# Attention steps taken by twos: which half of the TensorE array scores and value products use, and how often they trade

## The chip, the core and the metric

The kernel runs on one core of a Trainium2 chip. The metric is device time in microseconds (us) of one execution of the whole program. The time of the kernel before is the median of three runs, 1683.56 us (1682.72 to 1688.05).

## What is computed

One transformer block over 2048 tokens of width 512: a layer norm modulated by a condition vector, attention with 32 query heads of 16 dimensions that share a single key head and a single value head, a residual, a second modulated layer norm, a gated feed-forward layer of width 1792, and a second residual. The part that the change touches is the attention:

```python
q = (x @ wq).reshape(B, S, H, Dh).transpose(0, 2, 1, 3)
k = x @ wk
v = x @ wv
scores = jnp.einsum("bhqd,bkd->bhqk", q, k) * (Dh ** -0.5)
p = _softmax(scores, axis=-1)
o = jnp.einsum("bhqk,bkd->bhqd", p, v)
```

## The kernel before

**Stages.** A prologue (a plan of tokens, `PLAN`) makes the modulation vectors, the first layer norm, keys, values and the first queries. Then comes the main loop. Then a tail does what is left of the feed-forward layer on the whole array.

**The main loop** (lines 1106 to 1155) runs over 32 units, each a block of 256 queries by one group of 8 heads, and inside a unit over 16 steps `kb`, one for each tile of 128 keys. There are 512 steps, and each step has two halves, `n` = 0 and 1: 1024 half-steps. A half-step issues, in the order `ORDER` (line 57) and then a piece:

- `a0`, `a1`: two score tiles (PSUM tile `sa`, line 584) with queries along partitions, for a later unit. VectorE takes the row maximum of each into `mx` (line 599). The maxima later go into the query tile as an extra row, so that the exponentials can't overflow.
- `s0`, `s1`: two score tiles (PSUM tile `st`, line 634) with keys along partitions. ScalarE takes the exponential of each into `P` (line 642).
- `c`: the products of `P` with `V` (line 647), of a key tile two steps back (`vq`, `LAG` = 2). They gather over all 16 key tiles of a unit in one PSUM bank, `craw`.
- `piece` (line 1095): a few products of the rest of the block (queries `pq`, output projection `po`, gate and up `pgu`, down `pd`), handed out by `plan` and `places`.

**The array's two row sets.** Nearly all matmuls of the main loop use the TensorE array in 8 parts: 2 row sets (partitions 0 to 63 and 64 to 127) by 4 sets of 32 columns. The function `columns` (line 145) issues four matmuls, one for each set of columns. The row set comes from where the operands lie: `kp[64 * j:64 * j + 64]` in `a_product` (line 590) and `st_tile` (line 640), and `V[rs, t, :]` with `rs = slice(64 * j, 64 * j + 64)` in `pv` (lines 650 and 655). For a score tile `j` says which four of the eight heads it is. For a product with `V`, `j` says which 64 of the tile's 128 keys it adds up, so a product needs the score tiles of both `j`. A piece (`Couple.part`) uses both row sets, first the one that `pv` did not use last.

In the loop, `h` is taken from `sides(kb)`: the scores of a half-step use row set `1 - h`, and `pv` uses `sides(t)[second]` with its own, older key tile `t`.

**The exchange.** The matmuls that gather in `craw` come from both row sets, and one row set may only add to the bank when the other has finished. So after the products of one row set `hand_over` (line 159) issues a matmul of one column of zeros (`nought`) which raises the semaphore `turn`, and before the products of the other row set `take_over` (line 169) waits for it. Before the change this is done inside every step, between its two halves, and in the middle of every piece group.

Of the kernel before, what the change touches and what calls it, by code (L numbers as in the profile page):

```python
# [9 lines left out]
F32 = mybir.dt.float32  # L10
# [6 lines left out]
P = 128  # L17
# [38 lines left out]
A0 = 84  # L56
ORDER = "a0", "s0", "c", "a1", "s1"
LAG = 2
# [24 lines left out]
PBUFS = 4  # L83
# [6 lines left out]
def adaln_mqa_glu_kernel(  # L90
# [36 lines left out]
    def sbank(name):  # L127
        return psum["s"].tile([P, 512], F32, tag=name, name=name, bufs=psum["banks"][name])
# [16 lines left out]
    def columns(dst, l_, r_, start, stop):  # L145
        for c_ in range(0, P, 32):
            pe.matmul(dst[c_:c_ + 32], l_[:, c_:c_ + 32], r_, start=start, stop=stop)

    turn, done, side, open_ = nc.alloc_semaphore("turn"), [0], [0], [False]
# [4 lines left out]
    def behind(later, earlier):  # L154
        tc.add_manual_dep(later.ins, earlier.ins.name,
                          mybir.DependencyInfo(mybir.DependencyClass.Sync, mybir.DependencyReason.DATA),
                          reason="a bank that Tile doesn't follow")

    def hand_over():
        g, rs = 32 * (done[0] // 2 % 4), slice(64 * side[0], 64 * side[0] + 64)  # L160
        z = pe.matmul(raw_c["c"][g:g + 32, 0:1], nought[rs], nought[rs, 0:1], start=False, stop=False)
        if not done[0]:
            behind(z, nought_set)
        done[0] += 1
        z.then_inc(turn, 1)
        tc.add_to_no_dep_group("turn", z.ins)
        tc.no_tile_sem_insts.add(z.ins.name)

    def take_over(since=None):
        pe.wait_ge(turn, done[0] if since is None else since)  # L170
# [20 lines left out]
    class Couple:  # L191
# [3 lines left out]
        def part(self, n0, n1):  # L195
            if n0 == 0:
                for g in self.gs:
                    g.open()
            m = self.gs[0].n
            for n in range(n0, n1):  # L200
                if n == m:
                    take_over(self.since)
                for j in (1 - side[0], side[0]):
                    g = self.gs[j ^ (n >= m)]
                    l_, r_, *cut = g.term(n % m, slice(64 * j, 64 * j + 64))
                    columns(cut[0](g.bank) if cut else g.bank, l_, r_, n == 0, n == 2 * m - 1)
                if n == m - 1:
                    self.since = None
                    if open_[0]:
                        hand_over()  # L210
                        self.since = done[0]
            if n1 == self.n:
                for k, g in enumerate(self.gs):
                    g.end(g.bank, k == 1)
# [335 lines left out]
    P_ = {}  # L550
# [19 lines left out]
    def get_q(i):  # L570
        if i not in qps:
            b, o = units[i]
            assert (b * QU // QB, o) in qdone
            load_q(i)
        return qps[i]


    def sides(t):
        return (0, 1) if t % 2 == 0 else (1, 0)

    def spot(n):
        return n // 16, n // 8 % 2, n % 2, n // 2 % 4

    def a_product(i, n):
        qp = get_q(i)
        if i not in mxs:
            mxs[i] = wp.tile([P, 8, 2, 4], F32, tag="mx", name="mx", bufs=2)
        kc, qt, j, r = spot(n)
        sa = sbank("sa")
        l_, r_ = qp[64 * j:64 * j + 64, r, qt * P:(qt + 1) * P], kp[64 * j:64 * j + 64, kc * 512:(kc + 1) * 512]  # L590
        if first:
            pe.matmul(sa, l_, r_, start=True, stop=True)
        else:
            columns(sa, l_, r_, True, True)
        return i, n, sa

    def a_max(i, n, sa):
        kc, qt, j, r = spot(n)
        dve.tensor_reduce(mxs[i][:, 4 * j + r, qt, kc:kc + 1], sa, axis=AX.X, op=ALU.max)
        if i > 0 and n == 62:  # L600
            pend.append((i,))

    def a_tile(i, n):
        a_max(*a_product(i, n))

    pend = []

    def max_end(i):
        m16 = wp.tile([64, 32], F32, tag="m16", name="m16", bufs=4)
# [24 lines left out]
    def st_tile(i, t, pr, j, second):  # L634
        qp = get_q(i)
        if not second:
            P_[pr] = P2.tile([P, 2, 512], F32, tag=f"P{pr}", name=f"P{pr}", bufs=PBUFS)
        p_ = P_[pr]
        s_ = sbank("st")
        columns(s_, kp[64 * j:64 * j + 64, t * P:(t + 1) * P], qp[64 * j:64 * j + 64, 2 * pr:2 * pr + 2].rearrange("p r q -> p (r q)"),  # L640
                True, True)
        act.activation(p_[:, j], s_, AF.Exp, scale=0.25)
        Ps[i, t, 2 * j + pr] = p_[:, j]
# [3 lines left out]
    def pv(i, t, second):  # L647
        c_ = raw_c["c"]
        side[0] = j = sides(t)[second]
        rs = slice(64 * j, 64 * j + 64)  # L650
        start, stop = t == 0 and not second, t == NKB - 1 and second
        if second:
            take_over()
        for hh in range(4):
            z = pe.matmul(c_[32 * hh:32 * hh + 32, :], V[rs, t, :], Ps[i, t, hh][rs, :], start=start, stop=stop)
            if start and hh == 0 and i > 0:
                behind(z, raw_c["out"])
        open_[0] = not stop
        if not second:
            hand_over()  # L660
        raw_c["last"] = z
        if second:
            for hh in range(4):
                del Ps[i, t, hh]
            if stop:
                unit_end(i)
# [51 lines left out]
    for g in range(8):  # L718
        p_, r_, j = g // 4, g // 2 % 2, g % 2
# [65 lines left out]
    class Transposes:  # L785
        stage, n = "tr", 4

        def __init__(self, part, u):
            self.part, self.u = part, u
# [171 lines left out]
    alist = [(i, n) for i in range(len(units)) for n in range(64)]  # L961
# [32 lines left out]
    for tok in PLAN.split():  # L994
        name = tok.rstrip("0123456789")
# [8 lines left out]
    P2 = ctx.enter_context(tc.tile_pool(name="w2", bufs=1, reuse_waits="tile"))  # L1004
# [40 lines left out]
    def ready(pair, gs, i):  # L1045
        for g in gs:
            g.ready = i * NKB
        return [(pair, g) for g in gs]
# [54 lines left out]
    vq = []  # L1103
    lows = []

    for i, (b, o) in enumerate(units):
        if o == 0 and b == NQ - 1:
            ends = ffn_groups(NB - 1)
            first_rows.append(Couple(*ends[0][:2]))
        if o == 0 and b % 2 == 1 and b < NQ - 1:  # L1110
            blocks[b // 2] = ffn_groups(b // 2)
            wos, trs, _, es = blocks[b // 2]
            main.extend([*ready(b // 2, [Couple(*wos[:2]), trs[0], trs[2]], i), (None, len(es)), *ready(b // 2, es, i)])
        if o == 0 and b % 2 == 0 and b > 0:
            wos, trs, gs, _ = blocks.pop(b // 2 - 1)
            gs = [Couple(*wos[2:]), trs[1], trs[3], *gs]
            main.extend([*ready(b // 2 - 1, gs[:-KEPT], i), (None, KEPT), *ready(b // 2 - 1, gs[-KEPT:], i)])
        for kb in range(NKB):
            s = i * NKB + kb
            now[0] = s  # L1120
            if kb == NKB - QLEAD - 5 and i + 2 < len(units):
                get_q(i + 2)
            late, pend[:] = pend[:], []
            for z in [z for z in waits if z[0] <= s]:
                waits.remove(z)
                z[1]()
            rows = [max_end(*z) for z in late]
            an = A0 + 4 * s

            old, lows[:] = lows[:], []  # L1130
            for n, h in enumerate(sides(kb)):
                for z in ORDER:
                    k = int(z[1:] or 0)
                    if z[0] == "a" and an + 2 * k + 1 - h < len(alist):
                        a_tile(*alist[an + 2 * k + 1 - h])
                    if z == "c" and len(vq) >= LAG:
                        pv(*vq[0], n == 1)
                    if z[0] == "s":
                        st_tile(i, kb, k, 1 - h, n == 1)
                if n == 1:  # L1140
                    lows.extend(z() for z in rows)
                piece(s, n)
                if n == 0:
                    for z in old:
                        z()
            if len(vq) >= LAG:
                vq.pop(0)
            vq.append((i, kb))
            while wdone < nw:
                if wdone < nw - 4 and (wdone + 0.5) * WSTEPS > (s + 1) * (nw - 4):  # L1150
                    break
                if wdone >= nw - 4 and s < WLAST + 3 * (wdone - nw + 4):
                    break
                wjobs[wdone]()
                wdone += 1
    assert wdone == nw and len(qdone) == 4 * NB
    while run:
        piece(s, 1)
    while vq:
        for n in range(2):  # L1160
            pv(*vq[0], n == 1)
        vq.pop(0)
    while waits:
        now[0] += 1
        for z in [z for z in waits if z[0] <= now[0]]:
# [54 lines left out]
```

## Time and profile before

| | |
|---|---|
| median of the runs, us | 1683.56 |
| the profiled execution: its own time, us | 1685.55 |
| the profiled execution: span from first to last instruction, us | 1683.7 |
| mean granted TensorE clock | 0.99 |
| share of the span busy: PE, DVE, ACT, POOL | 98%, 85%, 77%, 36% |

PE is TensorE, DVE VectorE, ACT ScalarE, POOL GpSimd; PEld is the loading of weights into the array. A row of the timeline gives the start, the length until the last of its instructions ended, the engine, the line, the operation, the tiles written and read, the shape and how many instructions follow each other. A shape like `64*32` ahead of the operand is the part of the array that a matmul uses. A matmul's length has its way through the array in it, so how long a row set is taken is read from the distance of starts, not from the lengths. All matmuls of the helper stand under line 136.

### The profile page before, as it was taken

To read this page: it belongs to the slowest core of one execution; us is meant where nothing else is said; L and a number is where in the kernel's file an instruction comes from. 1 tells how busy PE (TensorE), PEld (TensorE's weight loads), DVE (VectorE), ACT (ScalarE), POOL (GpSimd) and SP (SyncE) were. 2 spreads that over 40 slices of the span, in tenths; PEclk is the share of its full clock that TensorE was granted. 3 is DMA by queue.
4 is the path that set the end of the run, shared out by engine and by line. 5 is a ranking of instruction groups with operands and counts; after the bars stand their busy time and mean duration, and the time that the engine had idled before them with its cause. 6 is when DMAs were issued, how large, how long until landed. Compare 5 with 4: busy or idle time off the path is not lost.

```text
span 1683.7 us, 87854 instructions
## 1 busy us (share of the span) xinstructions
PE 1644.5 (98%) x39747; PEld 974.6 (58%) x39747; DVE 1430.9 (85%) x2428; ACT 1295.4 (77%) x2335; POOL 610.5 (36%) x784
## 2 busy tenths in 40 slices
PE   6999999999999999999999999999999999999998
PEld 3335445454456666666656666666666666654443
DVE  7789999999999999999999999999999999912311
ACT  5548889888888888888888888888888888884100
POOL 4432445475033442222543232223543333132423
PEclk9989999999999999999999999999999999999999
DMA  7111333331011120101021110100121110011211
GB/s 242 57 62 28 103 114 96 98 96 40 21 61 41 57 70 15 41 28 28 28 77 53 47 45 15 41 24 27 38 78 49 45 53 16 24 47 52 88 51 38
DMA packets 86722, 94.05 MB, mean 56 GB/s; under 512 B 24916, under 2 KB 65868, under 8 KB 86348
## 3 DMA queue, kind: packets, MB, share of 16 engines
q1 hardware_dynamic: 86348, 88.44, 17.0%
q8 instruction: 311, 5.10, 1.2%
q14 instruction: 63, 0.52, 0.1%
HBM read 67.82 MB, written 16.24 MB: 50 GB/s over the span
## 4 chain that ended last, share of the span: by engine, by line
PE 83%; DVE 11%; ACT 2%; issue 1%; DMA 1%; POOL 0%; SPq 0%; POOLq 0%; ACTq 0%; DVEq 0%
PE craw L136 23%; PE sa L136 16%; PE pgu L136 14%; PE st L136 10%; DVE mx L136 9%; PE pd L136 6%; PE pgu L187 5%; PE pd L187 3%; PE po L136 2%; PE pq L136 2%; ACT P L136 1%; DMA xall<-in_A_x_dram 1%; ACT th L136 1%; DVE h2h L136 1%; DVE st L136 1%
## 5 line engine op out<-in xcount | busy, mean ns | idle before, releaser
L136 DVE TENSOR_REDUCE mx<-sa 128x1 f32<-128x512 f32 x2048 | 1291.5, 682 | 64.0 <-PE sa L136 29.1
L136 ACT ACTIVATE P<-st 128x512 f32<-128x512 f32 x2048 | 1175.2, 598 | 197.2 <-PE st L136 133.6
L136 PE MATMUL craw<-P,V 64*32 64x512 f32 x8192 | 1088.0, 598 | 0.2
L136 PE MATMUL sa<-kp,qp 64*32 64x512 f16 (+1 forms) x7940 | 826.6, 378 | 10.5 <-DVE mx L136 9.8
L136 PE MATMUL st<-qp,kp 64*32 64x512 f16 x8192 | 831.8, 379 | 4.8 <-ACT P L136 4.5
L136 PEld LDWEIGHTS <-kp 64*32 64x32 f16 x8192 | 323.9, 91 | 254.5 <-issue 102.2
L136 PEld LDWEIGHTS <-qp 64*32 64x32 f16 (+1 forms) x7940 | 284.4, 92 | 166.5 <-issue 82.4
L136 PE MATMUL pgu<-h2h,gw 64*32 64x512 f16 x5248 | 273.8, 376 | 1.0
L136 PEld LDWEIGHTS <-gw 64*32 64x32 f16 x7872 | 175.0, 92 | 59.4 <-issue 16.2
L136 PEld LDWEIGHTS craw<-P,V 64*32 64x32 f32 x8192 | 184.5, 105 | 15.0 <-issue 2.0
L136 PE MATMUL pgu<-h2l,gw 64*32 64x512 f16 x2624 | 165.3, 376 | 0.3 <-POOL h2l L357 0.3
L901 POOL TENSOR_SCALAR th<-th 128x512 f32<-128x512 f32 x41 | 25.4, 620 | 356.0 <-ACT th L136 300.2
L136 PE MATMUL craw<-nought 64*32 64x1 f16 x571 | 93.1, 163 | 0.0
L557 POOL MEMSET qp<- 32x1024 f16 x60 | 56.7, 945 | 83.3 <-PE st L136 80.8
L321 POOL TENSOR_SCALAR wst<-wst 128x512 f32<-128x512 f32 x46 | 28.5, 621 | 144.7 <-DMA wst<-in_B_w_up_dram 89.4
L187 PE MATMUL pgu<-h2h,gw 128*128 128x512 f16 x240 | 71.9, 379 | 1.5 <-DVE h2h L356 1.5
L136 PEld LDWEIGHTS <-nought 64*32 64x32 f16 x571 | 53.1, 93 | 34.2 <-issue 28.8
L895 ACT ACTIVATE th<-pgu 128x512 f32<-128x512 f32 x15 | 9.0, 597 | 82.1 <-PE pgu L187 82.1
L136 PE MATMUL pd<-wdh,gh 64*32 64x512 f16 x1152 | 70.4, 376 | 0.6 <-DVE t L136 0.2
L136 PE MATMUL pd<-wdl,gh 64*32 64x512 f16 x1152 | 70.3, 376 | 0.0
L136 PE MATMUL pd<-wdh,gl 64*32 64x512 f16 x1152 | 69.7, 376 | 0.0
L136 DVE COPY u<-pgu 128x512 f32<-128x512 f32 x41 | 28.0, 682 | 48.6 <-PE pgu L136 48.4
(160 smaller groups left out, 1426.8 us busy)
## 6 DMA issues: line engine op xcount, KB each, us to landing
gw<-wD SPq DMA_DIRECT2D x56, 512.0 KB
wD<-gw SPq DMA_DIRECT2D x14, 512.0 KB
wm<-in_w_mod_dram SPq DMA_DIRECT2D x6, 1024.0 KB
qp<-qD SPq DMA_DIRECT2D x192, 32.0 KB
qD<-q SPq DMA_DIRECT2D x16, 256.0 KB
xr<-in_A_x_dram SPq DMA_DIRECT2D x16, 256.0 KB
out_dram<-ot SPq DMA_DIRECT2D x16, 256.0 KB
raw<-cs SPq DMA_DIRECT2D x248, 16.0 KB
```

Source lines behind the costliest of these rows:

```text
L136: return (lambda *a, **k: keep(f_(*a, **k))) if pinned else f_
L187: pe.matmul(cut[0](self.bank) if cut else self.bank, l_, r_, start=(n == 0), stop=(n == self.n - 1))
L321: pool.tensor_scalar(w_, w_, SW, 0.0, op0=ALU.mult, op1=ALU.add)
L557: eng.memset(qp[j:j + 32], 0.0)
L895: act.activation(th, p_, AF.Tanh, scale=0.5 / (SH * SW))
L901: pool.tensor_scalar(th, th, 1.0, 1.0, op0=ALU.add, op1=ALU.mult)
```

## The change

Steps go by pairs. A step now issues one row set's scores for both key tiles of its pair (one tile in each half-step), and the next step the other row set's. The products with `V` do the same with the two key tiles of the pair before. The function `sides` turns over with each pair of steps where it turned over with each step. There is one exchange for each pair of steps, and one more at each unit's first product. The number of score tiles, exponentials, maxima, products and pieces is as before.

```diff
                 if n == m:
+                    assert self.since is not None or done[0] > self.marks
                     take_over(self.since)
...
                 if n == m - 1:
-                    self.since = None
+                    self.since, self.marks = None, done[0]
...
     def sides(t):
-        return (0, 1) if t % 2 == 0 else (1, 0)
+        return (0, 1) if t // 2 % 2 == 0 else (1, 0)
...
-        if i > 0 and n == 62:
+        seen[i] = seen.get(i, 0) + 1
+        if i > 0 and seen[i] == 64:
             pend.append((i,))
...
-            P_[pr] = P2.tile([P, 2, 512], F32, tag=f"P{pr}", name=f"P{pr}", bufs=PBUFS)
-        p_ = P_[pr]
+            P_[t % 2, pr] = P2.tile([P, 2, 512], F32, tag=f"P{pr}", name=f"P{pr}", bufs=PBUFS)
+        p_ = P_[t % 2, pr]
...
         side[0] = j = sides(t)[second]
         rs = slice(64 * j, 64 * j + 64)
         start, stop = t == 0 and not second, t == NKB - 1 and second
-        if second:
+        if second and t % 2 == 0:
             take_over()
...
         open_[0] = not stop
-        if not second:
+        if start or not second and t % 2 == 1:
             hand_over()
...
-            an = A0 + 4 * s
+            an = A0 + 4 * (s - kb % 2)
+            second = kb % 2 == 1
+            h = sides(kb)[second]
 
             old, lows[:] = lows[:], []
-            for n, h in enumerate(sides(kb)):
+            for n in range(2):
+                t = kb - kb % 2 + n
                 for z in ORDER:
                     k = int(z[1:] or 0)
-                    if z[0] == "a" and an + 2 * k + 1 - h < len(alist):
-                        a_tile(*alist[an + 2 * k + 1 - h])
-                    if z == "c" and len(vq) >= LAG:
-                        pv(*vq[0], n == 1)
+                    if z[0] == "a" and an + 4 * n + 2 * k + 1 - h < len(alist):
+                        a_tile(*alist[an + 4 * n + 2 * k + 1 - h])
+                    if z == "c" and vq:
+                        pv(*vq[n], second)
                     if z[0] == "s":
-                        st_tile(i, kb, k, 1 - h, n == 1)
+                        st_tile(i, t, k, 1 - h, second)
...
-            if len(vq) >= LAG:
-                vq.pop(0)
-            vq.append((i, kb))
+            if second:
+                vq[:] = [(i, kb - 1), (i, kb)]
...
-    while vq:
-        for n in range(2):
-            pv(*vq[0], n == 1)
-        vq.pop(0)
+    for n in range(4):
+        pv(*vq[n % 2], n > 1)
```

On TensorE, at the second half of the first step that has products: `P_1236` and `P_1249` are the exponentials of key tile 0, `P_1262` and `P_1275` (in the changed program) those of key tile 1, `kp` and `qp` keys and queries. Before, the products of this half-step are of key tile 0 again, on the other row set, and wait for the exchange:

```order
L136 MATMUL st<-qp,kp 32x512
L136 MATMUL craw<-P_1236,V 32x512 [waits turn]
L136 MATMUL craw<-P_1249,V 32x512
L136 MATMUL craw<-P_1236,V 32x512
L136 MATMUL craw<-P_1249,V 32x512
L136 LDWEIGHTS qp
```

Now, at the same place, they are of key tile 1, on the same row set as in the half-step before, and the zero matmul of the exchange stands behind them:

```order
L136 MATMUL st<-qp,kp 32x512
L136 MATMUL craw<-P_1262,V 32x512
L136 MATMUL craw<-P_1275,V 32x512
L136 MATMUL craw<-P_1262,V 32x512
L136 MATMUL craw<-P_1275,V 32x512
L136 LDWEIGHTS nought
L136 MATMUL craw<-nought 32x1
L136 LDWEIGHTS qp
```

The wait for `turn` has moved to the next step, and half of these waits and zero matmuls are gone.

On ScalarE, the exponentials of the first two steps of the main loop, as a piece of the difference. Each row is one tile; a name stands twice because the two `j` of a key tile share a buffer:

```order
 L136 ACTIVATE P_1249<-st 128x512
+L136 ACTIVATE P_1262<-st 128x512
+L136 ACTIVATE P_1275<-st 128x512
 L136 ACTIVATE P_1236<-st 128x512
 L136 ACTIVATE P_1249<-st 128x512
-L136 ACTIVATE P_1286<-st 128x512
-L136 ACTIVATE P_1299<-st 128x512
```

One row set's exponentials of key tiles 0 and 1 now stand ahead of the other row set's of both; before, key tile 0 was finished first.

More of the change, by code (lines that the diff above doesn't have):

```diff
@@ L604, in a_tile @@
         a_max(*a_product(i, n))
-    pend = []
+    pend, seen = [], {}
     def max_end(i):
```

## The prediction

> **What bounds the kernel now.** I read the page's head first, then the busy times by stretch, then the costliest groups, then one half-step in the timeline. From the page:
>
> ```profile
> span 1683.7 us, 87854 instructions
> PE 1644.5 (98%) x39747; PEld 974.6 (58%) x39747; DVE 1430.9 (85%) x2428; ACT 1295.4 (77%) x2335; POOL 610.5 (36%) x784
> ```
>
> PE's 98% says little, since pipelined matmuls count as busy while they wait in line. The stretches ahead of, in and behind the main loop (first products at 115.6 us, last at 1539.3) say more. The columns are the length, then busy time and count of each engine, then the clock:
>
> ```profile
> 0.00:116.00 116.00, 96.39 (x658) 40.83 (x666) 90.89 (x182) 52.36 (x85) 53.90 (x102) 0.89 0.39 131
> 116.00:1540.00 1424.00, 1411.72 (x38471) 870.23 (x38455) 1306.65 (x2190) 1229.40 (x2225) 508.37 (x631) 1.00 0.17 50
> 1540.00:1684.00 144.00, 136.38 (x630) 63.55 (x630) 33.33 (x56) 13.64 (x25) 48.24 (x52) 0.98 0.16 55
> L136 PE MATMUL craw<-P,V x8192: 586/589/1057, 115.6 to 1539.3; 64*32 64x512 f32 x200
> ```
>
> The change touches only the 1424 us in the middle: 1024 half-steps of 1.391 us. In them VectorE is busy 1306.65 us, 92%, at full TensorE clock. What fills VectorE and ScalarE, by the page's groups:
>
> ```profile
> L136 DVE TENSOR_REDUCE mx<-sa 128x1 f32<-128x512 f32 x2048 | 1291.5, 682 | 64.0 <-PE sa L136 29.1
> L136 ACT ACTIVATE P<-st 128x512 f32<-128x512 f32 x2048 | 1175.2, 598 | 197.2 <-PE st L136 133.6
> ```
>
> A half-step has two maxima and two exponentials, so 2 x 0.682 = 1.364 us of VectorE and 2 x 0.598 = 1.196 us of ScalarE. Now a half-step on TensorE, from the timeline:
>
> ```profile
> 516.72 0.46 PE L136 MATMUL pgu<-h2l,gw 64*32 64x512 f16 x8
> ...
> 516.94 0.43 PE L136 MATMUL sa<-kp,qp 64*32 64x512 f16 x4
> ...
> 517.00 0.61 PE L136 MATMUL craw<-P,V 64*32 64x512 f32 x4
> ...
> 517.15 0.42 PE L136 MATMUL st<-qp,kp 64*32 64x512 f16 x4
> ...
> 517.37 0.42 PE L136 MATMUL sa<-kp,qp 64*32 64x512 f16 x4
> ...
> 517.42 0.61 PE L136 MATMUL craw<-P,V 64*32 64x512 f32 x4
> ...
> 517.58 0.42 PE L136 MATMUL st<-qp,kp 64*32 64x512 f16 x4
> 517.67 1.21 ACT L136 ACTIVATE P<-st 128x512 f32<-128x512 f32 x2 [0.39 <-PE st L136]
> ...
> 517.80 0.42 PE L136 MATMUL pgu<-h2h,gw 64*32 64x512 f16 x4
> 517.85 0.16 PE L136 MATMUL craw<-nought 64*32 64x1 f16 x1
> 517.86 0.61 PE L136 MATMUL pgu<-h2h,gw 64*32 64x512 f16 x12
> ```
>
> This is the view that decides. Two streams run beside each other. On one row set the four score tiles start at 516.94, 517.15, 517.37 and 517.58, and the piece follows at 517.80: 0.86 us for four, so **0.215 us** for a tile. On the other row set the float32 products start at 517.00, their second pass at 517.42, and what stands behind them (the zero matmul) at 517.85: 0.85 us, so **0.425 us** a pass. The two streams take the same time, and each hides the other. A piece's matmuls in groups of eight, four for each row set, take 0.215 us on both at once. How many there are is read from the weights they load, one load for each matmul:
>
> ```profile
> L136 PEld LDWEIGHTS <-gw 64*32 64x32 f16 x7872 | 175.0, 92 | 59.4 <-issue 16.2 <-PE craw L136 1.7
> L136 PEld LDWEIGHTS <-gh 64*32 64x32 f16 x2304 | 54.1, 92 | 16.7 <-issue 4.2
> ...
> L136 PEld LDWEIGHTS <-a 64*32 64x32 f16 x1344 | 30.2, 92 | 9.9 <-issue 2.0 <-POOL a L713 0.7
> L136 PEld LDWEIGHTS <-gl 64*32 64x32 f16 x1152 | 29.3, 92 | 7.3
> ...
> L136 PEld LDWEIGHTS <-wdh 64*32 64x32 f16 x640 | 14.4, 93 | 2.7 <-issue 0.6 <-PE craw L136 0.6
> ```
>
> With 320 more for the queries' low weights (the third of three equal parts, two of which load `wdh`) it is 13,632, that is 1704 groups, 1.664 in a half-step. So TensorE needs 0.86 + 1.664 x 0.215 = 1.218 us in a half-step, VectorE 1.364 and a little more, and 1.391 passes. VectorE and TensorE are both close to the limit, VectorE closer.
>
> **The change, part by part.** First, what row set each operation gets. The scores of step `kb` use `1 - h` with `h = sides(kb)[second]`. The products handed out in that step are of the pair before, `kb - 2`, and use `sides(t)[second]`. The new `sides` turns over with each pair, so `sides(kb - 2)` is the opposite of `sides(kb)`:
>
> | step | scores on | products of | products on |
> |---|---|---|---|
> | 2 | 1 - 1 = 0 | tiles 0, 1 | 0 |
> | 3 | 1 - 0 = 1 | tiles 0, 1 | 1 |
> | 4 | 1 - 0 = 1 | tiles 2, 3 | 1 |
> | 5 | 1 - 1 = 0 | tiles 2, 3 | 0 |
>
> **They are always on the same row set.** Before, products came two steps behind with a `sides` of period two, and so always stood opposite. The built program says so too: in 1023 of 1024 half-steps the products now have the row set of the scores ahead of them. The same row set then serves four half-steps in a row, and the other one has only its half of the pieces.
>
> The sum for a half-step on the row set in use: four score tiles 4 x 0.215 = 0.86, two float32 passes 0.85, pieces 1.664 x 0.215 = 0.358, together 2.068 us. For 1024 of them: 2117.6 us. VectorE (1.364) and ScalarE (1.196) now have room, and no wait for them is late.
>
> What comes off is the overlap where the row set changes, once in four half-steps, 256 times. The next block's scores may start on the free row set while the old one ends. In the order of the program the next products would start 2.068 + 0.43 = 2.50 us after the last half-step's beginning. The bounds:
>
> - Least: nothing starts ahead of what stands before it in the program, so only the last piece's slot is shared: 0.215 us.
> - Most: only semaphores hold it. Products wait for the exchange. Its price is the distance from the zero matmul to the products behind the wait:
>
> ```profile
> 575.39 0.16 PE L136 MATMUL craw<-nought 64*32 64x1 f16 x1
> ...
> 575.64 0.67 PE L136 MATMUL craw<-P,V 64*32 64x512 f32 x3
> ```
>
> 0.25 us here. The old products end 0.43 + 0.85 = 1.28 us into the half-step, so the new ones start at 1.53 at best. The second reason comes to the same: `st` has two buffers, so the next `s0` waits for the exponential of the last half-step's `s0`, which starts at 0.215, is released 0.52 us later (517.15 to 517.67 above) and takes 0.598: 1.33, and the products stand one tile behind, 1.55. So 2.50 - 1.53 = 0.97 us at most.
>
> Does TensorE start work that stands far behind? In the timeline above the piece at 517.80 started ahead of the zero matmul at 517.85, which stands 18 instructions before it in the program (by the order list: eight for `sa`, eight for `st`, two of the piece). It does, across row sets, where nothing waits. 45 to 60 are needed here. I take 0.85, near the semaphores' bound: 256 x 0.85 = 218 us.
>
> The Trainium skill, "TensorE: Matmul & The Clock Gate", Part 3, says under what overlaps and what doesn't that matmuls start and end strictly in program order and that only weight loads are pulled ahead. By that rule the overlap would be the least one. This trace disagrees: the row at 517.80 starts before the row at 517.85 that precedes it.
>
> The exchanges: 571 zero matmuls become 347. One costs its row set the distance 517.85 to 517.86, 0.01 us, so 224 give 2 us; I cost them at nothing, between that and a wait of 0.25 each (56 us), which the dearer row set now covers, since scores and pieces follow the zero matmul on the same row set. Moved: the maxima of a unit are complete one step later, its two small reductions and four DMAs on SP's queue with them, and still some three longer steps before the scores that need them. `P` has four buffers and at most four are alive. The prologue and the tail (116 and 144 us) stay.
>
> Sum: 2117.6 - 218 = 1900 us for the middle in place of 1424: +476. The profiled execution took 1685.55 us, 2 us over the median of the runs. 1685.55 + 476 = 2161, I say **2160 us**.
>
> **The rivals.**
>
> *The reach is short.* If TensorE looks only about as far as the trace shows, the overlap lies between 0.215 and half the bound. At 0.215: 2117.6 - 55 = 2063, so 2324 us; at 0.45, 2264. For it: the rows above show a start 18 instructions ahead, not 45. Against: nothing in this program called for more. Chance 0.2.
>
> *More dead time.* Waits between scores and exponentials on one row set, or a clock that falls with half the array idle: the prologue's 0.89 is the lowest here. Over 2345 us. Chance 0.05.
>
> *Faster than before: the exchange was the bound.* The half-step takes 0.17 us more than TensorE's 1.218 now. If that were the exchange and scores could run inside the products' passes on one row set, the middle would fall to VectorE's 1306.65 us, a gain of 117: 1568 us. It decides from the point where a half-step on one row set takes less than 1.39 in place of 2.07. Against: the rows 516.94 to 517.80 show tiles of one row set in single file, and VectorE's 1.364 explains the 1.391. Chance 0.02.
>
> *The change doesn't do what it says*, scores and products stay opposite: the half-steps stay at 1.391, about 1684 us. The table of row sets speaks against it. Chance 0.01.
>
> **How the numbers follow.** Forecast with an overlap of 0.6 to 0.97: 2117.6 - 154 to - 248, so 2130 to 2225 us, chance 0.68; the rivals above 0.28; and 0.04 for something between 1690 and 2105 that I have not thought of. The range runs from 2105 (25 under the semaphores' bound, for the count of pieces and ends) to 2345 (20 over the least overlap, for the transposes, which I left out). About 0.3% can be told from no change: faster 0.02, same 0.01, slower 0.97.
>
> **What would show it.** Starts of `craw` passes and score tiles that no longer lie beside each other: `sa`, `st`, then `craw` twice, then `sa`, `st`, 1.71 us and the piece. DVE's busy time about the same 1430 us with its share near 66%. Every fourth half-step shorter by some 0.85 us: if by 0.2, the reach was short. Half-steps without pieces at 1.71. `nought` 347 times. It would be wrong if score tiles start while `craw` passes of the same row set run, or if the clock falls.

## The result, and the profile after

The changed kernel takes 2261.05 us (median of 4 runs, 2252.03 to 2270.56) against 1683.14 us: 1.343 times as long, 95% interval [1.336, 1.349]. The forecast was 2160 us with a range of 2105 to 2345. The profiled execution took 2263.25 us, its span is 2261.5 us. The ratios leave out one run of the experiments, which took 2303.49 us at a granted clock of 0.971 where the other three of its kernel took 2250.87 to 2255.07.

From the page of the changed kernel, the head and the two groups that filled VectorE and ScalarE before:

```profile
span 2261.5 us, 87583 instructions
PE 2229.6 (99%) x39523; PEld 1019.8 (45%) x39523; DVE 1514.6 (67%) x2428; ACT 1308.2 (58%) x2335; POOL 609.0 (27%) x784
...
L136 DVE TENSOR_REDUCE mx<-sa 128x1 f32<-128x512 f32 x2048 | 1374.6, 688 | 543.4 <-PE sa L136 498.2
L136 ACT ACTIVATE P<-st 128x512 f32<-128x512 f32 x2048 | 1185.8, 596 | 750.1 <-PE st L136 646.3
```

VectorE has waited 498 us for score tiles of TensorE, where it was 29 before, and ScalarE 646 us (134 before). But for 224 zero matmuls (39747 - 39523), each matmul, maximum and exponential is there as often as before. TensorE alone is the limit now: its own waits for maxima and exponentials add up to 8.6 us. Its 99% says as little as its 98% did.

By stretch, the middle of the changed kernel has 2000 us in place of 1424, and the two ends only 2 us more together:

```profile
0.00:116.00 116.00, 95.87 (x602) 39.65 (x606) 89.77 (x181) 51.18 (x83) 51.53 (x99) 0.87 0.40 131
116.00:2116.00 2000.00, 1996.25 (x38276) 916.98 (x38269) 1391.48 (x2192) 1243.41 (x2228) 509.24 (x634) 0.99 0.12 35
2116.00:2262.00 146.00, 137.53 (x651) 63.18 (x649) 33.37 (x56) 13.64 (x25) 48.19 (x52) 0.99 0.16 54
```

The timeline shows why. One half-step of the changed kernel, with a piece of two groups, on TensorE:

```profile
801.53 0.39 PE L136 MATMUL sa<-kp,qp 64*32 64x512 f16 x4
801.74 0.39 PE L136 MATMUL st<-qp,kp 64*32 64x512 f16 x4
801.96 0.60 PE L136 MATMUL craw<-P,V 64*32 64x512 f32 x4
801.98 0.40 PE L136 MATMUL pgu<-h2h,gw 64*32 64x512 f16 x4
802.39 0.60 PE L136 MATMUL craw<-P,V 64*32 64x512 f32 x4
802.41 0.40 PE L136 MATMUL pgu<-h2l,gw 64*32 64x512 f16 x4
802.82 0.39 PE L136 MATMUL sa<-kp,qp 64*32 64x512 f16 x4
803.03 0.39 PE L136 MATMUL st<-qp,kp 64*32 64x512 f16 x4
803.25 0.39 PE L136 MATMUL pgu<-h2h,gw 64*32 64x512 f16 x4
803.47 0.39 PE L136 MATMUL pgu<-h2l,gw 64*32 64x512 f16 x4
803.68 0.39 PE L136 MATMUL sa<-kp,qp 64*32 64x512 f16 x4
```

Read the starts: 801.53, 801.74, 801.96, 802.39, 802.82, 803.03, 803.25, 803.47, 803.68. That is one file on one row set: two score tiles, two passes of products, two score tiles, two groups of the piece, 2.15 us. The only rows beside it are the free row set's halves of the piece (801.98 and 802.41). Before, the score tiles at 516.94 to 517.58 lay beside the passes at 517.00 and 517.42.

And a change of row set. The last half-step of a block begins at 811.67, the next block's products start at 813.66:

```profile
811.67 0.41 PE L136 MATMUL sa<-kp,qp 64*32 64x512 f16 x4
811.89 0.41 PE L136 MATMUL st<-qp,kp 64*32 64x512 f16 x4
812.11 1.05 PE L136 MATMUL craw<-P,V 64*32 64x512 f32 x8
812.58 0.40 PE L136 MATMUL pgu<-h2l,gw 64*32 64x512 f16 x4
812.97 0.38 PE L136 MATMUL sa<-kp,qp 64*32 64x512 f16 x3
813.00 0.16 PE L136 MATMUL craw<-nought 64*32 64x1 f16 x1
813.01 0.40 PE L136 MATMUL pgu<-h2h,gw 64*32 64x512 f16 x4
...
813.23 0.39 PE L136 MATMUL sa<-kp,qp 64*32 64x512 f16 x4
...
813.45 0.38 PE L136 MATMUL st<-qp,kp 64*32 64x512 f16 x3
...
813.66 0.60 PE L136 MATMUL craw<-P,V 64*32 64x512 f32 x3
```

That is 1.99 us after the beginning, in place of 2.15 + 0.43 = 2.58 in the program's order: an overlap of 0.6 us, where I had counted on 0.85. The next block's first score tile starts at 813.23. It is not the exchange that holds the products, since the zero matmul of 813.00 would let them go at 813.25, by the 0.25 us from 575.39 to 575.64 in the trace of before. They start one `sa` and one `st` after 813.23. Over the whole trace, the first products of neighbouring half-steps start 2.10 us apart within a block and 1.52 us apart at a change of row set, on average.

### The profile page after: what moved, and what is told of

Read it like the earlier page. It is cut to its first block, busy times and chain, and to the rows that moved or that the text cites. A ratio compares the mean times of both kernels' runs of the same rounds, so it can differ in the third digit from the quotient of the medians.

```text
span 2261.5 us, 87583 instructions
## 1 busy us (share of the span) xinstructions
PE 2229.6 (99%) x39523; PEld 1019.8 (45%) x39523; DVE 1514.6 (67%) x2428; ACT 1308.2 (58%) x2335; POOL 609.0 (27%) x784
## 4 chain that ended last, share of the span: by engine, by line
PE 94%; DVE 3%; ACT 1%; issue 1%; DMA 0%; POOL 0%; SPq 0%; POOLq 0%; ACTq 0%; DVEq 0%
PE craw L136 31%; PE sa L136 20%; PE st L136 16%; PE pgu L136 11%; PE pd L136 5%; PE pgu L187 3%; PE pq L136 2%; PE po L136 2%; PE pd L187 2%; DVE mx L136 2%; PE pt L136 0%; DMA xall<-in_A_x_dram 0%; ACT P L136 0%; DVE st L136 0%; PE pk L136 0%
## 5 line engine op out<-in xcount | busy, mean ns | idle before, releaser
L136 DVE TENSOR_REDUCE mx<-sa 128x1 f32<-128x512 f32 x2048 | 1374.6, 688 | 543.4 <-PE sa L136 498.2
L136 PE MATMUL sa<-kp,qp 64*32 64x512 f16 (+1 forms) x7940 | 780.4, 380 | 6.3 <-DVE mx L136 6.2
L136 PE MATMUL st<-qp,kp 64*32 64x512 f16 x8192 | 775.2, 379 | 2.5 <-ACT P L136 2.4
L136 PE MATMUL pgu<-h2h,gw 64*32 64x512 f16 x5248 | 463.6, 380 | 0.1
L136 PEld LDWEIGHTS <-kp 64*32 64x32 f16 x8192 | 254.3, 93 | 340.3 <-issue 247.2
L136 PEld LDWEIGHTS craw<-P,V 64*32 64x32 f32 x8192 | 261.6, 107 | 164.2 <-PE craw L136 5.8
L136 PE MATMUL pgu<-h2l,gw 64*32 64x512 f16 x2624 | 258.5, 380 | 0.0
L136 PE MATMUL po<-woh,a 64*32 64x512 f16 x896 | 78.5, 380 | 0.0
L136 PEld LDWEIGHTS <-gh 64*32 64x32 f16 x2304 | 62.2, 91 | 30.0 <-issue 3.9
L910 POOL TENSOR_TENSOR gl<-th,gh 128x512 f16<-128x512 f32 x56 | 64.9, 1159 | 4.7
```

Source lines behind the costliest of these rows:

```text
L136: return (lambda *a, **k: keep(f_(*a, **k))) if pinned else f_
L910: pool.tensor_tensor(lo[:, to], th[:, of], hi[:, to], op=ALU.subtract)
```

## The experiments

My theory after the result: scores and products share a row set and go in single file; the overlap at a change of row set is smaller than I said, because TensorE doesn't start work so far ahead. The rivals: the order by twos costs the time; the exchange does; or semaphores set the overlap.

### The other row set for the scores

```diff
-            h = sides(kb)[second]
+            h = sides(kb)[not second]
```

> The changed kernel with one line altered: the scores go to the row set that the products don't use. Steps by twos, the lag of a pair and the 224 fewer exchanges stay. Theory (the shared row set costs everything): the half-steps come back to VectorE's bound, the middle takes 1400 to 1430 us in place of 1998, the whole 1660 to 1690 us, ratio to before 0.985 to 1.005. Rival (the order by twos, or the later use of the exponentials, costs the time, not the row set): it stays near 2261 us.

Measured: 1677.15 us, ratio 0.9955 [0.994, 0.997]. The middle, by stretch:

```profile
116.00:1534.00 1418.00, 1402.97 (x38247) 855.23 (x38231) 1305.29 (x2190) 1228.24 (x2226) 508.12 (x631) 1.00 0.17 50
```

The two streams lie beside each other again:

```profile
516.88 0.41 PE L136 MATMUL sa<-kp,qp 64*32 64x512 f16 x4
516.94 0.61 PE L136 MATMUL craw<-P,V 64*32 64x512 f32 x4
517.10 0.41 PE L136 MATMUL st<-qp,kp 64*32 64x512 f16 x4
```

VectorE is busy 1305 of 1418 us, as it was before the change. One `not` takes back the whole 578 us, with steps by twos and the 224 fewer exchanges kept. The shared row set is the cause, and this version is 0.45% faster than the kernel before.

### The kernel before, with scores and products on one row set

```diff
-                    if z[0] == "a" and an + 2 * k + 1 - h < len(alist):
-                        a_tile(*alist[an + 2 * k + 1 - h])
+                    if z[0] == "a" and an + 2 * k + h < len(alist):
+                        a_tile(*alist[an + 2 * k + h])
...
-                        st_tile(i, kb, k, 1 - h, n == 1)
+                        st_tile(i, kb, k, h, n == 1)
```

> The kernel before with its scores put on the row set of the products, nothing by twos, an exchange in each step. The row set then changes every 2 half-steps (512 times) and not every 4 (256 times). Theory (row set in single file, and each change of row set gives 0.62 us of overlap, as measured in the changed kernel): 1024 x 1.722 + 1704 x 0.2155 - 511 x 0.62 + 10 = 1823 us for the middle, about 2085 us in all (2060 to 2110). Rival (steps by twos are the cause): about 1684 us. Second rival (the overlap does not come from the changes of row set): no gain from more of them, about 2260 us or more.

Measured: 2103.41 us, ratio 1.2485 [1.2461, 1.2509]; the products run from 115.6 to 1958.5 us:

```profile
L136 PE MATMUL craw<-P,V x8192: 587/589/614, 115.6 to 1958.5; 64*32 64x512 f32 x200
```

So the loss comes without any steps by twos, and it is smaller, since the row set changes twice as often. From 1843 us the overlap is (1024 x 2.08 - 1843) / 511 = 0.56 us for each change, a little under the 0.62 I had put in: that is the value where a piece stands at the change, and some half-steps have none.

### An exchange at every half-step

```diff
-        if second and t % 2 == 0:
+        if not start:
             take_over()
...
-        if start or not second and t % 2 == 1:
+        if not stop:
             hand_over()
```

> The changed kernel with an exchange after every half-step's products, also between two that use the same row set: 1051 zero matmuls in place of 347, and a wait ahead of nearly every half-step's products. Theory (an exchange is covered by the scores and pieces that stand between, and costs its row set 0.01 us): 704 x 0.01 = 7 us more, 2255 to 2280 us. Rival (an exchange costs the 0.25 us from the zero matmul to the products behind the wait): some 700 x 0.25 = 175 us more, about 2435 us.

Measured: 2254.04 us (2253.01 without the run of 2303.49), ratio 1.3371 [1.3344, 1.3397]. That is 1 us below the range I gave, and the interval overlaps that of the changed kernel, [1.336, 1.349]. The 175 us of the rival aren't there. The medians can't show 7 us, since the runs of the changed kernel differ by 18. The traces can, as far as one execution of each goes. The products of the two kernels, the changed one first:

```profile
L136 PE MATMUL craw<-P,V x8192: 586/589/1060, 119.9 to 2118.2; 64*32 64x512 f32 x200
```

```profile
L136 PE MATMUL craw<-P,V x8192: 586/589/634, 119.7 to 2110.0; 64*32 64x512 f32 x200
```

It is 1998.3 against 1990.3 us. But the changed kernel's profiled execution holds a stretch at a lower clock that this one hasn't (PEclk is the third number from the end):

```profile
260.00:300.00 40.00, 38.98 (x450) 14.25 (x434) 20.66 (x34) 19.04 (x35) 10.10 (x12) 0.66 0.14 42
```

That is 40 x 0.34 = 13.6 us. Without it the changed kernel has 1984.7, and 704 more exchanges cost 5.6 us, about 0.008 each. On a shared row set the exchange is covered.

### How far ahead TensorE starts work

A kernel of its own: k groups of near matmuls on row set 0, one far group on row set 1 behind them, nothing to wait for. Ahead of each trial stand 40 matmuls of the whole array, left out here.

```diff
+        for i in range(k):
+            for c in cols:
+                keep(nc.tensor.matmul(near[c:c + 32], w[:64, c:c + 32], m[:64], start=(i == 0), stop=(i == k - 1)))
+        for c in cols:
+            keep(nc.tensor.matmul(far[c:c + 32], w[64:, c:c + 32], m[64:], start=True, stop=True))
```

> A kernel of its own that leaves out the whole computation and copies its input to the output: k groups of matmuls (64x512, float16, one 64x32 part of the array each; first four column sets in a group, then one) on row set 0, and behind them one group on row set 1, nothing to wait for between them. How long after the first near one does the far one start? Theory (TensorE sees past 12 matmuls that have not started, no more): four column sets: at once for k up to 4, then 0.215 us later for each further group (k = 8: 0.86, k = 12: 1.72); one column set: at once up to 13, k = 16: 0.65, k = 20: 1.5, k = 24: 2.4, k = 40: 5.8. Rival (32 matmuls with their weight loads, and the semaphores set the overlap in the kernel): four column sets at once up to k = 8, k = 12: 0.65; one column set at once up to 32, k = 40: 1.5. Second rival (strictly in program order): (k - 1) x 0.215 from the start.

Measured, four column sets with k = 4 and k = 8, then one column set with k = 8 and k = 12:

```profile
54.40 0.40 PE L44 MATMUL near<-m,w 64*32 64x512 f16 x4
54.45 0.40 PE L46 MATMUL far<-m,w 64*32 64x512 f16 x4
...
84.19 1.26 PE L44 MATMUL near<-m,w 64*32 64x512 f16 x20
85.08 0.40 PE L46 MATMUL far<-m,w 64*32 64x512 f16 x4
85.28 0.82 PE L44 MATMUL near<-m,w 64*32 64x512 f16 x12
...
115.91 1.25 PE L44 MATMUL near<-m,w 64*32 64x512 f16 x5
116.79 0.39 PE L46 MATMUL far<-m,w 64*32 64x512 f16 x1
117.00 0.81 PE L44 MATMUL near<-m,w 64*32 64x512 f16 x3
126.47 2.11 PE L44 MATMUL near<-m,w 64*32 64x512 f16 x9
128.22 0.39 PE L46 MATMUL far<-m,w 64*32 64x512 f16 x1
128.43 0.81 PE L44 MATMUL near<-m,w 64*32 64x512 f16 x3
```

With four column sets it is as expected: at once for k = 4, 0.89 us late for k = 8, with 12 near matmuls still to start. With one column set the theory fell. At k = 12, where I expected no delay, the far one is 1.75 us late, and only **3** near ones are still to start. It isn't 12 in all; it looks like 3 for each part of the array, the four column sets making 12. "Strictly in program order" falls with the first two rows.

### Three at each part?

The same kernel with one or two near column sets in several orders, and the far matmul on row set 1 and the fourth column set. `sets` is the list of the near matmuls' column sets.

```diff
+        for c in sets:
+            seen[c // 32] += 1
+            keep(nc.tensor.matmul(near[c:c + 32], w[:64, c:c + 32], m[:64], start=(seen[c // 32] == 1),
+                                  stop=(seen[c // 32] == used[c // 32])))
+        c = 96
+        keep(nc.tensor.matmul(far[c:c + 32], w[64:, c:c + 32], m[64:], start=True, stop=True))
```

> A kernel of its own that leaves out the whole computation and copies its input to the output: near matmuls on one or two column sets of row set 0, then one far matmul on row set 1 and column set 3. How long after the first near one does the far one start? Theory (three wait at each part, the fourth holds up the rest): 3 or 4 on one set at once, 5: 0.215, 6: 0.43; on two sets in turn 4 each at once (6 wait), 5 each 0.215, 6 each 0.43; 5 on one and then 3 on the other 0.215; 4 and 4 at once; 4 and then 5 0.215; 1 on the second and then 7 on the first 0.645. Rival (three may wait in a whole row set, twelve only as four at a time): two sets in turn with 4 each would start late, by some 0.4 us.

Measured, of the eleven orders three: 4 on each of two sets in turn, 5 on each in turn, and 5 on one and then 3 on the other:

```profile
65.31 0.39 PE L47 MATMUL near<-m,w 64*32 64x512 f16 x2
65.33 0.39 PE L50 MATMUL far<-m,w 64*32 64x512 f16 x1
...
75.01 0.61 PE L47 MATMUL near<-m,w 64*32 64x512 f16 x4
75.25 0.39 PE L50 MATMUL far<-m,w 64*32 64x512 f16 x1
...
95.07 0.62 PE L47 MATMUL near<-m,w 64*32 64x512 f16 x3
95.32 0.39 PE L50 MATMUL far<-m,w 64*32 64x512 f16 x1
```

At once with 6 waiting on two parts, 0.24 us late with one more on each, and 0.25 late where a single part has one too many, though the other has room. All eleven came within 0.03 us of what was expected. A part holds one matmul at work and three waiting; a fourth stands at the head of the line and stops all that is behind it, for other parts too.

### The piece's row sets in the other order

Does this set the overlap in the kernel? At 812.58 above the free row set's piece started only when the products' second pass had freed a place, and the next scores stood behind two such pieces.

```diff
-                for j in (1 - side[0], side[0]):
+                for j in (side[0], 1 - side[0]):
```

> The changed kernel with the two row sets of a piece issued in the other order: first the row set that the scores and products use, then the free one. Theory (three matmuls may wait at each part of the array, the fourth holds up all that stands behind it, so what the free row set gets at a change of row set depends on what stands ahead of it in the program): the free row set's piece and the next block's scores start later, the next products at 2.16 us from the last half-step's beginning in place of 1.97, an overlap of 0.43 in place of 0.62 at the some 197 changes that have a piece: 37 us more, about 2290 us where no stretch is at half clock. Rival (the semaphores, the exchange or the two st buffers, set the overlap): no change, 2250 to 2262 us.

Measured: 2286.99 us, ratio 1.3594 [1.3562, 1.3626]. The last half-step of a block begins here at 1226.82, one `st` before 1227.03:

```profile
1227.03 0.39 PE L136 MATMUL st<-qp,kp 64*32 64x512 f16 x4
1227.25 1.03 PE L136 MATMUL craw<-P,V 64*32 64x512 f32 x8
1228.11 0.38 PE L136 MATMUL sa<-kp,qp 64*32 64x512 f16 x3
1228.12 0.16 PE L136 MATMUL craw<-nought 64*32 64x1 f16 x1
1228.12 0.40 PE L136 MATMUL pgu<-h2h,gw 64*32 64x512 f16 x4
...
1228.56 0.38 PE L136 MATMUL sa<-kp,qp 64*32 64x512 f16 x3
...
1228.99 1.03 PE L136 MATMUL craw<-P,V 64*32 64x512 f32 x8
```

The free row set's piece starts at 1228.12, 0.87 us behind the products' first pass, where it was 0.47 (812.11 to 812.58); the next products start 2.17 us after the beginning in place of 1.99. The products run from 118.2 to 2140.9 us, 2022.7: 38 us more than the 1984.7 of the changed kernel, with 37 expected. What stands ahead in the program, and not a semaphore, sets the overlap.

### Where the better version's gain comes from

The first experiment's kernel with an exchange at every half-step.

```diff
-            h = sides(kb)[second]
+            h = sides(kb)[not second]
...
-        if second and t % 2 == 0:
+        if not start:
             take_over()
...
-        if start or not second and t % 2 == 1:
+        if not stop:
             hand_over()
```

> The kernel with scores opposite to the products and steps by twos (1677 us, 0.9955 of before), with an exchange after every half-step's products: 1051 zero matmuls. Theory (its gain over the kernel before comes from the exchanges that it saves, whose waits are not wholly covered where the row sets run beside each other): the gain goes, ratio to before 1.000 to 1.010. Rival (the gain comes from the order by twos): the ratio stays at 0.994 to 0.997.

Measured: 1692.57 us, ratio 1.0048 [1.0035, 1.006]. The gain goes. This kernel and the first experiment's differ in the exchanges alone, 1051 zero matmuls against 347: (1.0048 - 0.9955) x 1684 / 704 gives 0.022 us for an exchange where the row sets run beside each other. At that price the 224 exchanges saved are worth 5 of the 7.6 us that the first experiment gained. The other 2.6 us lie within the two intervals, so a gain from the order by twos itself isn't shown.

## Why the prediction was right, and by how much not

**Same row set, single file: right.** The table of row sets in the prediction carried it. The two experiments that exchange only the row sets take the loss away (0.9955) and bring it into the kernel before (1.2485).

**The half-step's sum: right to 0.6%.** 2.08 us (0.215 and 0.43 from the starts at 801.53 to 803.68: 4 x 0.2155 + 2 x 0.43 + 1.664 x 0.2155) where 2.068 was forecast; over 1024 half-steps 12 us.

**What VectorE and ScalarE take: read too high.** The prediction takes 0.682 and 0.598 us, the lengths of one record, but the records overlap. The same rows say how long the groups were busy: 1291.5 / 2048 = 0.631 us for a maximum and 1175.2 / 2048 = 0.574 us for an exponential, so a half-step took 1.26 us of VectorE and not 1.364. The sum of the forecast doesn't use it, and both had room. But "VectorE's 1.364 explains the 1.391" doesn't hold, and what limits the kernel before isn't settled here. It isn't the exchange: 571 of them at 0.022 us are 13 us. VectorE's busy time also didn't stay at about 1430 us: it came to 1514.6, 67% of the span. 83 of the 84 us are the maxima's, which stand further apart now and so overlap less.

**The overlap at a change of row set: mis-sized.** It was the step "I take 0.85, near the semaphores' bound: 256 x 0.85 = 218 us", after "It does, across row sets, where nothing waits". Measured: the products' starts span 1998.3 us; the single file would have 1023 x 2.08 = 2128; with the 13.6 us of the lower clock the overlap is 2128 - 1998 + 14 = 144 us, 0.56 a change. 74 us of the 101 by which the result passed the forecast are this term; the half-step's sum and the clock give 12 and 14 more. The reach of 45 to 60 instructions that it needed isn't there: three matmuls may wait at a part. So the result lies in the range, but above the 2130 to 2225 us that had the chance of 0.68. The rival "the reach is short", with 0.2, named the cause, but its overlap went up to half the bound only, some 0.48: 0.56 lies between it and the forecast's 0.6 to 0.97, and gives 2161 + 74 = 2235 us by itself. That the result comes so near the rival's 2264 us is luck, by the 26 us of the other two terms. The trace of before could show only that work starts ahead at all, since there both row sets have nearly the same load (0.86 and 0.85 us).

The Trainium skill, "TensorE: Matmul & The Clock Gate", Part 3, has matmuls start strictly in program order. The far matmul that starts 0.05 us after the first of 16 near ones (54.40 and 54.45) disagrees, as the trace of before did. Behind a full part nothing starts: the far one at 85.08 stood 0.89 us behind near ones for full parts, with its own parts idle.

**The clock: not in the forecast's sum.** The prediction has a falling clock as a rival, over 2345 us, and as a sign of being wrong. It did fall, for 27 us (270 to 297 us, PEclk 0.50), and cost 13.6 us in the profiled execution. The mean clock of 0.986 there is the second lowest of the four runs (0.983 to 0.991), and their times fall as it rises, from 2270.56 to 2252.03. It isn't this kernel's alone: with an exchange at every half-step, the run of 2303.49 us had a clock of 0.971, the other three 0.992 to 0.995, and the profiled one of them kept its full clock at 270 to 297 us. In both traces few pieces stand there, and TensorE waits 1.0 us for an exponential just ahead (until 269.30 and 269.62). So these two don't bring the clock down each time, and the cause stays open.

**The exchanges: right to cost at nothing here.** There are 347 zero matmuls in place of 571, 224 fewer and not half. One costs about 0.008 us on a shared row set. With the row sets beside each other it is about 0.022.

**The moved maxima, exponentials and buffers: right.** TensorE's waits for maxima and exponentials didn't grow: 6.2 and 2.4 us in the whole trace, where they were 9.8 and 4.5. VectorE and ScalarE wait for TensorE.

## What to carry to other kernels

When a change alters which part of the array an operation uses, write down the part of each operation for one period, before and after, with the lag between producer and consumer in it: a period of four with a lag of two turned "opposite" into "same". Price a part by the distance between starts on it, not by the length of a record and not by an engine's busy share, which moved from 98% to 99% while the time grew by a third. And don't count on TensorE to reach past a full part: what is to run beside it must stand in the program before the fourth matmul that waits there.

## What the runs showed of the hardware that was not expected

- A 64x32 part of the array takes one matmul at work and three waiting. The next one for that part holds up everything behind it, also for parts with nothing to do: 3 near matmuls left at one part (k from 4 to 40), 12 at four (k from 4 to 12). No run tests whether the two row sets of one column set have three places each or share them.
- In single file on one row set, the pass of a 64x512 float32 matmul is 0.43 us and the next operation follows without a gap, also between float32 and float16 (801.96, 802.39, 802.82).
